# Local attention and gated feed-forward on one core: the first Q/K products on 64x32 tiles from uncast weights, and engine orders given as lists

## The chip, the core and the metric

The kernel runs on one NeuronCore of a Trainium2 chip. The metric is the device time of one execution in microseconds (us); lower is better. A core has TensorE (PE in the profile; PEld is its weight loads), VectorE (DVE), ScalarE (ACT), GpSimd (POOL) and SyncE (SP), each with an instruction stream of its own. They wait for each other through semaphores, and every stream is executed in the order in which it was written. SP and ACT also start DMA transfers here.

## What is computed

The input x has 2048 tokens of 448 values in bfloat16. Four layers follow each other: attention (A), feed-forward (B), and both again with the same weights. Each adds to x what it makes of the layer-normed x. Attention has 16 heads of 28 values; a token looks at itself and at seven tokens before it, two apart. The feed-forward is the product of two projections to 1792 values, projected back, without an activation function.

```python
def _A_ref(x, wqkv, wo):
    B, S, D = x.shape
    H = 16; Dh = D // H
    W, dil = 8, 2
    qkv = (x @ wqkv).reshape(B, S, 3, H, Dh).transpose(2, 0, 3, 1, 4)
    q, k, v = qkv[0], qkv[1], qkv[2]
    ...
    logits = jnp.einsum("bhsd,bhswd->bhsw", q, kg) * Dh ** -0.5
    logits = jnp.where(mask[None, None, :, :], logits, -1e9)
    attn = _softmax(logits, axis=-1)
    o = jnp.einsum("bhsw,bhswd->bhsd", attn, vg)
    return o.transpose(0, 2, 1, 3).reshape(B, S, D) @ wo

def _B_ref(x, w_gate, w_up, w_down):
    return ((x @ w_gate) * (x @ w_up)) @ w_down

x = x + _A_ref(_layernorm(x), wqkv, wo)
x = x + _B_ref(_layernorm(x), w_gate, w_up, w_down)
x = x + _A_ref(_layernorm(x), wqkv, wo)
x = x + _B_ref(_layernorm(x), w_gate, w_up, w_down)
```

## The kernel before

All of x stays in SBUF (`x_sb`), as 16 blocks of 128 tokens, with even tokens in blocks 0 to 7 and odd ones in 8 to 15, so that a token's eight keys are neighbours. Four blocks make a chunk. The names in the code give layer and chunk: `A00` is attention of layer 0, chunk 0; `B10` is the feed-forward of layer 1, chunk 0. `SEQ` lists the jobs: A00 A01 B10 A02 B11 A03 B12 A20 and so on. A chunk of one layer thus overlaps with chunks of others.

**Norm** (`ln_chunk`). For each block VectorE takes statistics (L751, L753), ScalarE the reciprocal root of the variance for two blocks at a time (L754, L756), and VectorE writes the normed block to `xn_sb` (L772). The block then goes, transposed, to `xnTa` (attention) or `xnTb` (feed-forward). For the chunks in `PE_T` (chunks 0, 1 and 2 of layer 0) PE transposes it (L781, four matmuls of 128 columns a block) and ScalarE or VectorE copies it from PSUM (L787). All other blocks are transposed by a DMA that SP issues (L775).

**Q and K** (`qk_chunk`, `twin`, L818). The 448 rows of the contraction are split into seven steps of two 64-row halves; the two halves of a step are two matmuls that PE runs side by side, one for K and one for Q. A unit covers four heads: seven steps, 14 matmuls of 512 columns, into a pair of PSUM banks. Between step 3 and step 4 the halves swap their targets, and a semaphore wait stands there (`crossed`). Four heads of 28 values are spread over 128 columns, 32 a head. The weights therefore aren't used as they lie in HBM. They are staged in `hT`, which the feed-forward needs later only, and cast into `WQK` (L705, 12 copies on ScalarE, VectorE or GpSimd, whichever the scheduler picks). For the two chunks in `FULLQ` (00 and 01) all four units are full; for later chunks the fourth Q group lies in the gaps of the other columns, and a small DMA per 28 rows (`QX`) moves it into place. ScalarE or VectorE copies the pair to `qk` (L872).

**Attention** goes by groups of 240 queries. V is made by the same `twin` (L818) and copied (L925). Scores are 64 small matmuls of 28 rows by 64 columns (L958); ScalarE takes the exponent (L970), VectorE or GpSimd multiplies by a mask (L979). The second product is 64 matmuls on tiles of 64 rows by 32 columns (L997). Its sums come along as a 29th row, are spread by VectorE (L1021 to L1024) and inverted on ScalarE (L1026, L1027); VectorE multiplies (L1047) into `oT`. The output product (`y_blocks`, L834) is added to x by VectorE (L1065).

**Feed-forward** (`b_chunk`). Gate and up are two matmuls side by side, seven steps for 128 of the 1792 values (L1095). ScalarE copies the gate (L1101), VectorE multiplies it with up (L1104) into `hT`, and the down product (L834) is added to x. The last blocks of the last chunk use whole 128-row matmuls (L1116).

**Loads.** At the start SP and ACT issue chunk 0 of x in two loads of 224 KB, WV and the Q/K weights in four pieces each; SP then issues the other three chunks of x, wo, and gate, up and down weights, each load of these last three waiting for the one before it. While nothing else can run, PE executes warm-up products on zeroed data (L692), 18 first of all and 30 at lowest priority.

**What sets the order.** Every operation is added to a list with engines it may run on, an estimate of its duration, what it depends on and a priority. `Sched.schedule` then plays the kernel through with these estimates: an engine that is free takes the ready operation with the best priority, and PE also asks for free PSUM banks. What comes out is a fixed instruction stream for each engine. `TUNE` shifts the priority of most of the 1372 operations, and ties some to an engine:

```python
shift, eng = TUNE.get(op.idx, (0.0, -1))
op.prio += shift
if eng >= 0:
    op.engs = (self.ENGS[eng],)
```

Of the kernel before, what the change touches and what calls it, by code (L numbers as in the profile page):

```python
# [8 lines left out]
D = 448  # L9
H = 16  # L10
DH = 28
# [18 lines left out]
PE_T = ("00","01","02")  # L30
# [9 lines left out]
WQK_ENGS = ("act", "dve", "pool")  # L40
# [6 lines left out]
TUNE = {  # L47
# [229 lines left out]
class Sched:  # L277
    ENGS = ("pe", "act", "dve", "pool", "sp")
    PE_LAT = 200.0
    TO_PE = 22.0  # L280
    LAT = 35.0
    SAME = 30.0
    SELF_LAT = 180.0
    TAIL = {"pe": 0.0, "act": 112.0, "dve": 90.0, "pool": 80.0, "sp": 0.0}
    BEGIN = {"pe": 1120.0, "act": 820.0, "dve": 900.0, "pool": 800.0, "sp": 800.0}
    SWITCH = 175.0
# [289 lines left out]
def build(nc, A_x, A_wqkv, A_wo, B_w_gate, B_w_up, B_w_down, out):  # L576
# [46 lines left out]
    def one(fn, key=None):  # L623
        return [(fn, key)]
# [630 lines left out]
```

## Time and profile before

| what | value |
|---|---|
| median of 3 runs | 395.74 us (395.45 to 395.81) |
| the profiled execution | 395.34 us |
| its span, first to last instruction | 393.5 us |
| PE busy | 383.4 us (97%) |
| VectorE busy | 268.7 us (68%) |
| ScalarE busy | 182.8 us (46%) |
| GpSimd busy | 8.9 us (2%) |
| moved by DMA | 21.74 MB |

Rows of the profile name the line, the engine, the operation and what it writes from what (`ps` is PSUM), then how many. A pair of numbers ahead of a row is its start and its length in us. In brackets or behind an arrow stands what ended the idle time before it. A matmul's shape, such as 64*128, is rows by columns of the tile of the array that it uses. PE's matmuls are pipelined, so a row's length includes the drain of its last matmul, and the mean of one is longer than the distance between two.

### The profile page before, as it was taken

The numbers are of one execution on the slowest core, as the hardware profiler recorded it, in microseconds if no ns is written. First come the engines' busy times: TensorE is split into PE (matmuls) and PEld (weight loads), VectorE is DVE, ScalarE is ACT, GpSimd is POOL, SyncE is SP. The second block draws the span as 40 slices with busy tenths as digits, with TensorE's granted clock in tenths as the row PEclk, the third lists the DMA queues.
The fourth block names the chain that finished last, engine by engine and source line by source line (L and its number), as shares of the span: only waits on it lengthen the run. The fifth ranks groups of instructions, "written<-read, shape, count | busy, mean of one in ns | idle before, by whom it ended". The sixth has DMA issues, their size and how long they took to land.

```text
span 393.5 us, 12725 instructions
## 1 busy us (share of the span) xinstructions
PE 383.4 (97%) x5678; PEld 208.5 (53%) x5678; DVE 268.7 (68%) x577; ACT 182.8 (46%) x297; POOL 8.9 (2%) x29
## 2 busy tenths in 40 slices
PE   8999978999999999999999989999999999999997
PEld 6545544445545454455445545577545555544555
DVE  5996999997996375367874678843689893244323
ACT  4788775554536442464334543333646442134110
POOL 6110000000000000000000000000000000000000
DMA  8645473524230072000330002510003204100002
GB/s 273 189 91 132 109 110 105 85 49 50 48 42 15 13 97 55 2 13 4 66 68 16 16 3 50 72 28 13 27 26 72 27 2 93 45 5 2 23 2 72
DMA packets 50766, 21.74 MB, mean 55 GB/s; under 512 B 41912, under 2 KB 49816, under 8 KB 50712
## 3 DMA queue, kind: packets, MB, share of 16 engines
q1 hardware_dynamic: 49720, 19.95, 25.5%
q8 instruction: 45, 0.74, 0.8%
q10 hardware_dynamic: 992, 0.98, 0.7%
q14 instruction: 9, 0.07, 0.1%
HBM read 8.43 MB, written 1.84 MB: 26 GB/s over the span
## 4 chain that ended last, share of the span: by engine, by line
PE 92%; DVE 3%; DMA 2%; issue 1%; ACT 1%; ACTq 0%
PE ps L1095 43%; PE ps L834 26%; PE ps L818 16%; PE ps L958 2%; PE ps L997 2%; PE ps L1116 1%; DMA hT<-in_A_wqkv_dram 1%; DMA xnTb<-xn_sb 1%; DVE xn_sb L772 1%; DVE hT L1104 1%; ACT g_sb L1101 0%; ACTq L631 0%; DVE E_sb L979 0%; PE ps L781 0%; DVE qk L872 0%
## 5 line engine op out<-in xcount | busy, mean ns | idle before, releaser
L1095 PE MATMUL ps<-xnTb,WGU 64*128 64x512 bf16 x1568 | 178.4, 376 | 1.2 <-DMA xnTb<-xn_sb 0.9
L1095 PEld LDWEIGHTS ps<-xnTb,WGU 64*128 64x128 bf16 x1568 | 85.1, 94 | 84.5 <-issue 6.1
L1101 ACT ACTIVATE g_sb<-ps 128x512 bf16<-128x512 f32 x112 | 66.0, 596 | 110.2 <-PE ps L1095 86.4
L1104 DVE TENSOR_TENSOR hT<-g_sb,ps 128x512 bf16<-128x512 bf16 x112 | 75.8, 683 | 53.6 <-ACT g_sb L1101 50.6
L834 PE MATMUL ps<-WD,hT 64*128 64x448 bf16 x840 | 85.5, 349 | 0.1
L834 PEld LDWEIGHTS ps<-WD,hT 64*128 64x128 bf16 x840 | 43.9, 94 | 35.5 <-DVE hT L1104 0.6
L1065 DVE TENSOR_TENSOR x_sb<-x_sb,ps 128x448 bf16<-128x448 bf16 x62 | 35.8, 614 | 26.2 <-PE ps L834 26.2
L818 PE MATMUL ps<-xnTa,WQK 64*128 64x512 bf16 (+1 forms) x448 | 47.7, 356 | 0.0
L970 ACT ACTIVATE E_sb<-ps 128x1024 bf16<-128x1024 f32 (+1 forms) x36 | 33.6, 977 | 14.3 <-PE ps L958 13.9
L772 DVE TENSOR_SCALAR xn_sb<-x_sb,mv,rstd 128x512 bf16<-128x512 bf16 (+1 forms) x64 | 35.5, 581 | 6.2 <-ACT rstd L756 6.1
L751 DVE BATCH_NORM_STATS2 st<-x_sb 128x6 f32<-128x448 bf16 x64 | 37.4, 611 | 2.3 <-DMA x_sb<-in_A_x_dram 2.3
L818 PEld LDWEIGHTS ps<-xnTa,WQK 64*128 64x128 bf16 x448 | 23.5, 94 | 19.4 <-DVE qk L872 0.5
L834 PE MATMUL ps<-wo_g,oT 64*128 64x448 bf16 x256 | 30.5, 350 | 1.5 <-issue 1.5
L818 PE MATMUL ps<-WV,xnTa 64*128 64x448 bf16 (+1 forms) x252 | 28.5, 340 | 0.7 <-DVE hT L1104 0.4
L872 ACT ACTIVATE qk<-ps 128x1024 bf16<-128x1024 f32 (+1 forms) x23 | 21.5, 948 | 14.0 <-PE ps L818 13.9
L754 ACT ACTIVATE lnv<-mv,eps_sb 128x2 f32<-128x2 f32 x32 | 9.5, 300 | 32.7 <-DVE mv L753 32.7
L979 DVE TENSOR_TENSOR E_sb<-E_sb,MK 128x1024 bf16<-128x1024 bf16 (+2 forms) x39 | 23.2, 610 | 1.3 <-ACT E_sb L970 1.2
L1047 DVE TENSOR_TENSOR oT<-ps,R_sb 128x448 bf16<-128x448 f32 (+2 forms) x38 | 21.0, 597 | 2.8 <-ACT R_sb L1027 2.7
L1026 ACT ACTIVATE R_sb<-R_sb 128x960 f32<-128x960 f32 (+1 forms) x18 | 17.3, 961 | 11.4 <-DVE R_sb L1024 11.4
L872 DVE CAST qk<-ps 128x1024 bf16<-128x1024 f32 (+1 forms) x9 | 9.9, 1102 | 16.1 <-PE ps L818 16.1
L834 PEld LDWEIGHTS ps<-wo_g,oT 64*128 64x128 bf16 x256 | 12.6, 94 | 12.8 <-issue 1.9
L818 PEld LDWEIGHTS ps<-WV,xnTa 64*128 64x128 bf16 x252 | 12.2, 94 | 10.8 <-PE ps L818 1.6
(45 smaller groups left out, 179.2 us busy)
## 6 DMA issues: line engine op xcount, KB each, us to landing
out_dram<-x_sb SPq DMA_DIRECT2D x15, 112.0 KB, 1.7
WGU<-in_B_w_gate_dram SPq DMA_DIRECT2D x7, 224.0 KB, 3.4
WGU<-in_B_w_up_dram SPq DMA_DIRECT2D x7, 224.0 KB, 3.7
WD<-in_B_w_down_dram SPq DMA_DIRECT2D x14, 112.0 KB, 2.1
x_sb<-in_A_x_dram SPq DMA_DIRECT2D x3, 448.0 KB, 7.1
qk<-qk SPq DMA_DIRECT2D x24, 28.0 KB
xnTb<-xn_sb SPq DMA_TRANSPOSE x32, 3.1
hT<-in_A_wqkv_dram SPq DMA_DIRECT2D x2, 224.0 KB, 5.2
```

What stands on the lines that cost most here:

```text
L751: sc.add("dve", one(lambda E, B=B: E.bn_stats(st6[:, B, :], x_sb[:, B, :]), ("bn", li, B)), 525.0, deps=[("x", li - 1, B)] + ([("xn", li - ...
L772: sc.add("dve", one(lambda E, B=B, dst=dst, src=src: E.tensor_scalar(dst, src, mv[:, B, 0:1], rstd[:, B:B + 1], ALU.subtract, ALU.mult), ( ...
L818: parts[0 if s < 3 else 1][1].append((lambda E, w=w, c=c, lo=lo, st=st, sp_=sp_: E.matmul(u["out"](w), u["lhs"](w, c, lo, lo + 64), u["rhs ...
L834: ins.append((lambda E, w=w, c=c, lo=lo, st=st, sp_=sp_: E.matmul(outs(w), lhs(w, c, lo), rhs(w, c, lo), start=st, stop=sp_), keys[w] if s ...
L872: return E.activation(dst, src, ACT.Copy) if hasattr(E, "activation") else E.tensor_copy(dst, src)
L970: return E.activation(E_sb[:, slot, 2 * hp:2 * hp + 2, 0:w], ps[:, b0:b0 + 2, 0:w], ACT.Exp, scale=SCALE)
L979: return E.tensor_tensor(e, e, m, ALU.mult)
L1047: return E.tensor_tensor(dst, src, rec, ALU.mult)
L1065: sc.add("dve", one(lambda E: E.tensor_tensor(x_sb[:, B, :], x_sb[:, B, :], ps[:, bk[w], 0:D], ALU.add), ("x", li, B)), dve_est(D), deps=[ ...
L1095: ins.append((lambda E, u=u, k=k, w=w: E.matmul(u["out"](w), WGU[64 * w:64 * w + 64, k, 128 * u["fc"]:128 * u["fc"] + 128], X[64 * w:64 * ...
L1101: sc.add("act", one(lambda E, gs=gs, bk=bk: E.activation(g_sb[:, gs, 0:n], ps[:, bk[0], 0:n], ACT.Copy), ("G", li, jp, fc)), act_est(n), d ...
L1104: sc.add("dve", one(lambda E, gs=gs, bk=bk, fc=fc: E.tensor_tensor(hT[:, fc, hs, h0:h1], g_sb[:, gs, 0:n], ps[:, bk[1], 0:n], ALU.mult), ( ...
```

## The change

1. For chunks 00 and 01 the Q/K products take their weights from the staging area. Each matmul of a step becomes four on tiles of 64 rows by 32 columns: 28 columns of one head and the first four of the next, whose results no one reads. A unit has 56 matmuls in place of 14, with the same seven steps. These units wait for the staged weights and not for the casts. The end of the staging area gets four zeroed columns.
2. The 12 casts, now for later chunks only, wait for the normed block 3, have a priority of their own, and may run on ScalarE and VectorE but not on GpSimd. `WQK` loses its eighth column group.
3. Chunk 0 of x comes in four loads of 112 KB, one block each, two on SP and two on ACT.
4. Chunk 2 of layer 0 is transposed by DMA (`PE_T` has two chunks).
5. The scheduler's model of PE gets a delay for instructions that aren't fetched yet (`fetch_delay`); some estimates and latencies change.
6. `TUNE` is empty. `ORDER` gives, for each engine, the complete list of operations in the order to execute; the scheduler only works out the banks and checks that each can run.
7. Buffers that are overwritten wait for all of their readers, where they waited for the last unit's.

In the new streams PE has 41 warm-up products ahead of the first transpose (35 before), then 1, 1 and 5 between and behind the transposes of chunk 0. It has 5998 matmuls in all, for 5678: 448 on 64x32 tiles stand for 112, and 16 transposes are gone. VectorE gets five casts directly after the fourth normed block and the copy of one transposed block.

```diff
-PE_T = ("00","01","02")
+PE_T = ("00", "01")
-WQK_ENGS = ("act", "dve", "pool")
+WQK_ENGS = ("act", "dve")
+WQK_P = -18.6
...
-TUNE = {
...
+TUNE = {}
+ORDER = {
+    "pe": [
+        37, 38, 39, 40, 41, 42, 43, 44, 45, 46, 47, 48, 49, 50, 51, 52, 53, 54, 55, 56, 57, 58, 59, 60, 61, 62, 63, 64, 65, 66, 67, 68, 69, 70, 71, 72,
+        73, 74, 75, 76, 77, 142, 145, 78, 151, 79, 148, 80, 81, 82, 83, 84, 229, 221, 223, 222, 219, 224, 217, 220, 218, 175, 169, 172, 166, 230, 232,
...
+    ASK, NEED, FETCH = 164, 440, 2500.0
...
+    def fetch_delay(self, now, est, n):
+        a, self.fetched = self.fetched, self.fetched + n
+        z, late = self.fetched, 0.0
+        k = int((a - self.NEED) // 256) + 1
+        while k >= 0 and 256 * k + self.NEED < z:
+            if k in self.arrive and 256 * k + self.NEED >= a:
+                late = max(late, self.arrive[k] - (now + late + est * (256 * k + self.NEED - a) / n))
+            k += 1
+        k = max(0, int((a - self.ASK) // 256) + 1)
+        while 256 * k + self.ASK < z:
+            if k not in self.arrive:
+                ask = now + late + est * max(0.0, 256 * k + self.ASK - a) / n
+                self.arrive[k] = max(ask + self.FETCH, self.arrive.get(k - 1, 0.0) + 1300.0)
+            k += 1
+        return late
...
+                if ORDER:
+                    op = self.ops[ORDER[e][len(order[e])]] if len(order[e]) < len(ORDER[e]) else None
+                    if op is None or op not in pend[e] or self.ready_at(op, e) > now + 1e-6:
+                        continue
...
-    load_x(0, (0, 1, 2), "sp", 2400.0, -60)
-    load_x(0, (1, 2, 2), "act", 3000.0, -60)
+    load_x(0, (0, 1, 4), "sp", 2400.0, -60)
+    load_x(0, (1, 2, 4), "act", 2400.0, -60)
+    load_x(0, (2, 3, 4), "sp", 2800.0, -59.9)
+    load_x(0, (3, 4, 4), "act", 2800.0, -59.9)
...
+    sc.add("pool", one(lambda E: E.memset(stage[:, 8 * D:8 * D + 4], 0.0), "c_stg"), 100, prio=-45)
...
-            sc.add(WQK_ENGS, one(fn, ("wqk", c, w)), dict(zip(("act", "dve", "pool"), ests)), deps=[("stg", c), "c_wqk0"], prio=-28)
+            sc.add(WQK_ENGS, one(fn, ("wqk", c, w)), dict(zip(("act", "dve", "pool"), ests)), deps=[("stg", c), ("xn", 0, 3)], prio=WQK_P)
...
+                for b in range(u.get("cols", 0)):
+                    ins.append((lambda E, w=w, c=c, lo=lo, st=st, sp_=sp_, b=b: E.matmul(
+                        u["out"](w)[32 * b:32 * b + 32], u["lhs"](w, c, lo, lo + 64)[b], u["rhs"](w, c, lo, lo + 64), start=st, stop=sp_, tile_position=(lo, 32 * b)),
+                        u["keys"][w] if sp_ and b == 3 else None))
...
             def lhs(which, dc, lo, hi):
+                if full:
+                    o = 2 * D * dc + (0 if which else D) + 4 * DH * c
+                    return [stage[lo:hi, o + DH * b:o + DH * b + 32] for b in range(4)]
                 return WQK[lo:hi, dc, c if halved else 4 * which + c, :]
...
-            return dict(bk=bk, out=out, lhs=lhs, rhs=rhs, n=n, deps=WQKR, keys=(("Kps", li, j, c), ("Qps", li, j, c)), c=c)
+            return dict(bk=bk, out=out, lhs=lhs, rhs=rhs, n=n, deps=[("stg", k) for k in range(4)] + ["c_stg"] if full else WQKR, keys=(("Kps", li, j, c), ("Qps", li, j, c)), c=c, **({"cols": 4} if full else {}))
...
-            readersA.setdefault((li, B), []).extend([("Kps", li, j, 3), ("Qps", li, j, 3)])
+            readersA.setdefault((li, B), []).extend([(n, li, j, c) for c in range(4) for n in ("Kps", "Qps")])
```

More of the change, by code (lines that the diff above doesn't have):

```diff
@@ L46 @@
 FILL = 30
-TUNE = {
[172 rows of a table removed]
+TUNE = {}
+ORDER = {
[15 rows of a table added]
+    ],
+    "act": [
[12 rows of a table added]
+    ],
+    "dve": [
[20 rows of a table added]
+    ],
+    "pool": [
+        23, 31, 24, 32, 27, 21, 28, 29, 19, 25, 26, 20, 33, 34, 30, 22, 35, 36,
+    ],
[6 rows of a table added]
+    ],
 }
@@ L394, in schedule @@
                 best = None
+                if ORDER:
+                    op = self.ops[ORDER[e][len(order[e])]] if len(order[e]) < len(ORDER[e]) else None
+                    if op is None or op not in pend[e] or self.ready_at(op, e) > now + 1e-6:
+                        continue
+                    if op.acquire is not None and self.pick_banks(op.acquire, now) is None:
+                        continue
+                    best = op
                 cands = []
-                for op in pend[e]:
+                for op in () if ORDER else pend[e]:
                     r = self.ready_at(op, e)
@@ L460, in schedule @@
                     mode = op.mode
+                    est += self.fetch_delay(now, est, 2 * len(op.ins))
                 op.start, op.end = now, now + est
@@ L597, in build @@
     qk = sb([128, 2, 4, S], bf, "qk")
-    WQK = sb([128, 4, 8, 128], bf, "WQK")
+    WQK = sb([128, 4, 7, 128], bf, "WQK")
     WV = sb([128, 4, D], bf, "WV")
@@ L800, in crossed @@
                 xid[0] += 1
-                tags = [("cross", xid[0], h) for h in (0, 1)]
-                ins = ins[:-2] + [(fn, [t] + ([k] if k is not None else [])) for (fn, k), t in zip(ins[-2:], tags)]
+                tags = [("cross", xid[0], h) for h in range(2 * cols)]
+                ins = ins[:-2 * cols] + [(fn, [t] + ([k] if k is not None else [])) for (fn, k), t in zip(ins[-2 * cols:], tags)]
                 nextk = tags
@@ L1102, in b_chunk @@
                        deps=[("Gps", li, jp, fc), prev], release=[(bk, 0)], prio=prio)
-                war = hslot_users.get((hs, "prev"), WQKR)
+                war = hslot_users.get((hs, "prev"), STGR)
                 sc.add("dve", one(lambda E, gs=gs, bk=bk, fc=fc: E.tensor_tensor(hT[:, fc, hs, h0:h1], g_sb[:, gs, 0:n], ps[:, bk[1], 0:n], ALU.mult), ("H", li, jp, fc)), dve_est(n),
                        deps=[("G", li, jp, fc), ("Ups", li, jp, fc)] + war, release=[(bk, 1)], prio=prio)
-        xslot_users[hs] = (xslot_users[hs] if part == "b" else []) + [("Gps", li, jp, FC - 1), ("Ups", li, jp, FC - 1)]
+        xslot_users[hs] = (xslot_users[hs] if part == "b" else []) + [(n, li, jp, fc) for fc in range(FC) for n in ("Gps", "Ups")]
         users = []
```

53 lines of the change are left out of this document (28 added, 25 removed), and 222 rows, old and new, of tables (ORDER, TUNE).

## The prediction

> **What bounds the kernel now.** I read the page first, then TensorE's busy time by stretches, then its waits, then the start in order of time.
>
> ```profile
> span 393.5 us, 12725 instructions
> PE 383.4 (97%) x5678; PEld 208.5 (53%) x5678; DVE 268.7 (68%) x577; ACT 182.8 (46%) x297; POOL 8.9 (2%) x29
> ```
>
> TensorE (PE) is busy for 97% of the span. A gain must come from work taken off PE, from the time before its first useful product, or from its pauses. The stretches (length, then busy time and count of each engine, granted clock, DMA) size these three:
>
> ```profile
> 11.26:60.77 49.51, 45.81 (x1042) 24.29 (x1043) 44.27 (x113) 39.74 (x61) 1.27 (x1) 1.00 0.55 119
> 60.77:391.10 330.33, 328.01 (x4572) 177.33 (x4572) 217.04 (x446) 137.76 (x226) 0.00 (x0) 1.00 0.21 38
> 11.26:391.10 379.84, 373.82 (x5614) 201.62 (x5614) 261.31 (x558) 177.50 (x286) 1.27 (x1) 1.00 0.25 48
> 391.10:393.50 2.40, 0.01 (x1) 0.00 (x0) 0.39 (x1) 0.00 (x0) 0.00 (x0) 1.00 0.23 72
> ```
>
> So the span is 11.26 us of start, 373.8 us of PE work, 3.7 us of pauses up to the first gate product (60.77), 2.3 us of pauses after it, and a tail of 2.4. The profiled execution took 395.34 us, 1.84 more than its span, and 0.4 less than the median of 395.74. The pauses by cause:
>
> ```profile
> PE ps L834 <- issue: 1.5, 1, 1.5
> PE ps L958 <- DVE E_sb L979: 1.4, 1, 1.4
> PE ps L1095 <- DMA xnTb<-xn_sb: 0.9, 1, 0.9
> PE ps L997 <- DVE v_sb L925: 0.8, 1, 0.8
> ```
>
> Three of the four belong to one place, 53 to 61 us, where VectorE is late with masks, V and the norm of layer 1. VectorE is busy 44.27 of 49.51 us in that stretch: it is PE's close second there, and everything I claim about the start must pass it.
>
> **The start, part by part.** Before, it goes so:
>
> ```profile
> 1.12 6.86 PE L692 MATMUL ps<-warm 128*128 128x256 bf16 x35 [1.12 <-DVE warm L663]
> 1.32 0.93 SPq L631 DMA_DIRECT2D WV<-in_A_wqkv_dram  x2
> 4.34 1.15 DVE L751 BATCH_NORM_STATS2 st<-x_sb 128x6 f32<-128x448 bf16 x2 [2.33 <-DMA x_sb<-in_A_x_dram]
> 6.59 0.30 DVE L753 BATCH_NORM_AGGREGATE mv<-st 128x2 f32<-128x6 f32 x2
> 6.81 0.70 DVE L772 TENSOR_SCALAR xn_sb<-x_sb,mv,rstd 128x512 bf16<-128x512 bf16 x2
> 7.43 0.27 DVE L705 COPY WQK<-hT 128x448 bf16<-128x448 bf16 x1
> 7.61 0.71 ACT L705 ACTIVATE WQK<-hT 128x112 bf16<-128x112 bf16 x1 [0.87 <-DMA hT<-in_A_wqkv_dram]
> 7.63 3.43 POOL L705 COPY WQK<-hT 128x448 bf16<-128x448 bf16 x6 [2.53 <-DMA hT<-in_A_wqkv_dram]
> 8.60 1.54 DVE L772 TENSOR_SCALAR xn_sb<-x_sb,mv,rstd 128x512 bf16<-128x512 bf16 x2 [0.90 <-ACT rstd L756]
> 10.07 0.73 DVE L787 COPY xnTa<-ps 128x512 bf16<-128x512 bf16 x2
> 10.20 0.40 PE L781 MATMUL ps<-ident,xn_sb 128*128 128x128 bf16 x4
> 13.73 4.91 PE L818 MATMUL ps<-xnTa,WQK 64*128 64x512 bf16 x44
> 18.57 1.07 PE L781 MATMUL ps<-ident,xn_sb 128*128 128x128 bf16 x16
> ```
>
> *x in four loads.* The 112 KB loads of WD landed a median 2.1 us after issue, the first 224 KB of x after 3.5:
>
> ```profile
> WD<-in_B_w_down_dram SPq DMA_DIRECT2D x14, 112.0 KB, 2.1
> x_sb<-in_A_x_dram SPq DMA_DIRECT2D x1, 224.0 KB, 3.5
> hT<-in_A_wqkv_dram ACTq DMA_DIRECT2D x2, 224.0 KB, 5.5
> ```
>
> Block 0 thus lands 0 to 1.4 us earlier; I take 0.7, the middle, as two loads still share the engines. Each queue issues one load more, so WV, the staged weights and x chunks 1 to 3 issue about 0.47 us later (0.93 for two issues). The staged weights then land by about 3.3 + 5.5 = 8.8 us; that must beat PE's need, below.
>
> *Casts out of the way.* The pair of norms at 8.60 waited for a reciprocal root behind ScalarE's first cast, and ran at 0.77 us each while GpSimd copied (the earlier pair: 0.35 each). Without casts the four norms follow each other: statistics from 3.6, 2.5 us for four blocks as before, then four norms of 0.35. They end near 7.6, not 10.15.
>
> *But PE does not come then.* Its order is fixed: 41 warm-up products now stand ahead of the first transpose, not 35.
>
> ```profile
> L692 PE MATMUL ps<-warm 128*128 128x256 bf16 x27 | 5.9, 420 | 1.1 <-DVE warm L663 1.1
> ```
>
> That row covers the first 6.8 us: 27 products at 0.21 us spacing, their slow phase, though the code plans 18. The other eight of the 35 fit the rest at about 0.11. So 41 end at 1.12 + 27 x 0.212 + 14 x 0.107 = 8.3 us. Sixteen transposes at 1.07/16 and two warm-ups between them take 1.3 us, to 9.7. The last transposed block is copied by VectorE (0.4 us) to about 10.3; five warm-ups and six V products fill the time. The useful stream begins at about 10.25 instead of 11.26: **-1.0 us**. The weights (8.8) are there. Most of the 2.5 us that the norms win is lost to warm-ups.
>
> *First products on 64x32 tiles.* A unit was 14 matmuls, two row halves by seven steps; now each is four matmuls of 32 columns, 56 in all. Before, 44 matmuls took 4.91 us, 22 steps of 0.22. The nearest rows for 64x32 tiles are the attention's second product:
>
> ```profile
> L997 PE MATMUL ps<-E_sb,v_sb 64*32 64x64 bf16 x1024 | 10.9, 195 | 0.8 <-DVE v_sb L925 0.8
> ```
>
> and from the chain that ended last (start, length, how many):
>
> ```profile
> 22.24 2.26 PE ps L818 x20
> ...
> 27.41 0.27 PE ps L997 x32
> ...
> 31.03 0.61 PE ps L997 x64
> ...
> 40.65 0.76 PE ps L834 x8
> ...
> 44.89 0.64 PE ps L958 x64
> ```
>
> Twenty full products took 2.26 us, two at a time, so one alone streams 512 columns in 0.226. Thirty-two matmuls of 72 columns, one after another, would need 32 x 72/512 x 0.226 = 1.02 us; they took 0.27: nearly four run at once, at least. Eight pairs of load and matmul issue in 8 x 0.61/64 = 0.076 us, well inside a step of 0.22. So the step stays at 0.22 us if all eight tiles stream together, and doubles if only four do: 0 to +12.3 us for the 56 steps of two chunks. I take +0.3, nearest to the row, whose 0.27 us is set by issue as much as by streaming; no row shows a limit at four.
>
> [...]
>
> *Chunk 2 transposed by DMA.* Sixteen PE transposes go: **-1.0 us** (18.57 row), and with them four PSUM copies. SP issues four transposes instead, as it does for chunk 3 (the second row is the landing of those four):
>
> ```profile
> 24.78 3.95 SPq L775 DMA_TRANSPOSE xnTa<-xn_sb  x3
> DMA to landing us min/median/max: 2.4/3.6/5.2
> ```
>
> They take 1.3 us each to issue, queued among the gate and up loads. The changed order asks for chunk 2 after about 16.4 us of PE work, at 27 us. VectorE's last norm of that chunk comes near 23.5, and such transposes landed 2.4 to 5.2 us after issue: 26 to 28.7, a pause of 0 to 1.7. I put 0.5 of it into the pauses below.
>
> *The casts, moved.* Twelve casts now follow the fourth norm on ScalarE and VectorE alone. VectorE gets five at once, about 1.3 us (its one before took 0.27), after the copy that ends at 10.3. Its statistics of chunk 1 begin at 11.5, not 10.72: VectorE loses 0.8 us where PE wins 1.0. GpSimd's one mask goes to VectorE too, and is in the count below.
>
> *The orders.* From there the lists decide.
>
> ```profile
> 10.72:55.17 44.45, 42.51 (x952) 22.57 (x950) 39.21 (x102) 36.37 (x58) 1.61 (x2) 1.00 0.51 120
> 56.46 4.07 DMA xnTb<-xn_sb
> ```
>
> Before, VectorE worked 39.2 us from the statistics of chunk 1 (10.72) to the fourth layer-1 norm (55.17), and idled 5.2; that norm's DMA transpose took 4.1, and the first gate product came at 60.77. The changed order has nearly the same work on VectorE in between, 91 instructions for 92: gone are four half masks and a half Q/K copy (about 1.9 us), new are a mask, a cast and two output products split off (1.8). So the norm ends at 11.5 + 39.1 = 50.6 without idling, 55.8 with the old idle time. I take a quarter of it, 51.9, since the masks, V and sums come to VectorE earlier while it still has norms to do; that choice weighs most in the sum. The gate product can then start at 51.9 + 4.1 + 0.2 = 56.2.
>
> PE's work ahead of it in the new order, by the chain's rows: 56 steps of 64x32 (12.3), 16 transposes (1.1), 84 + 28 products with cast weights, full and half (11.1), 84 + 14 V products (8.6), 48 output products (4.6), scores and second products (6.2), together 43.9 us. With 0.8 us of pauses on the way, PE is there at 10.25 + 43.9 + 0.8 = 55.0 and waits 1.2. The pauses up to there are 2.0 us (3.7 before), **-1.7**.
>
> Behind it PE is full, as before.
>
> ```profile
> 231.10 0.71 PE L958 MATMUL ps<-qk 28*64 28x64 bf16 x64
> 231.73 0.68 PE L997 MATMUL ps<-E_sb,v_sb 64*32 64x64 bf16 x64
> ...
> 234.59 0.55 PE L834 MATMUL ps<-wo_g,oT 64*128 64x448 bf16 x3 [1.46 <-issue]
> ```
>
> The 1.5 us "issue" pause stands in the middle of a stage, behind 128 short products: its next instructions weren't there. The fetch model moves such bursts apart; the gain is 0 to 1.5, and the change adds 320 matmuls to fetch. I take 1.2 left of 2.3, **-1.1**. The order ends on the same 42 products: the tail costs the same. The other edits (semaphores, latencies, wider waits for buffers long read) cost nothing while PE's work covers them; the lists already contain their effect.
>
> **Sum:** 395.34 - 1.0 - 1.0 - 1.7 - 1.1 + 0.3 = 390.8 for a profiled execution like this one; the 0.4 up to the median stays inside the range.
>
> **Rivals.**
>
> *Half the tiles wait (slower).* If moving data or PSUM writes let only four of eight tiles stream, each of 56 steps costs 0.22 more: 390.8 + 12.0 = 402.8. It decides from 4.8/56 = 0.09 us a step on. For it: no row has 512 columns on such tiles. Against: the 72-column row already reaches four, limited by issue. 10%.
>
> *Weight loads show.* If a tile's load waits for the matmul in that tile, a step grows by up to eight pairs' issue, 0.076 us: +4.3 in place of 0.3, 394.8. Steps with two halves hide their loads entirely (PE's busy time is full of products, PEld's 53% lies beside it), which speaks against. [...] 10%.
>
> *VectorE is the bound.* With its old 5.2 us of idling the fourth norm ends at 55.8, the gate product starts at 60.0, and PE's remaining 328.9 us (373.8 - 1.0 - 43.9), 1.2 of pauses, tail and 1.84 give 394.3: most of the gain is given back at layer 1. For it: 44.27 of 49.51 busy, and a later start of chunk 1. Against: what it waits for comes earlier. 14%.
>
> *The orders miss.* The lists have no slack; one more pause such as the present 1.5 in each of three layers would give 395.3. 8%.
>
> **Chances.** Forecast 58% (388.6 to 393). Its low end: no idling on VectorE (-1.2) and the warm-ups' slow phase shorter by a third (27 to 18 products, -1.0). The high end, 395.3, takes in VectorE, the exposed loads and the missed orders, and leaves out the doubled step. 0.2% (0.8 us) is about what a measurement of this kernel can tell from no change. Faster by more (below 394.95): forecast, 11 of VectorE's 14 and 7 of the 18 in the two cases near 395, 76%; within it: 3 and 6, 9%; slower: 5 and the 10, 15%.
>
> **What would show it.** PE's first V product near 10.2 and its first 64x32 product near 10.5, behind a 41-long row of warm-ups; 224 products of chunk 0 in about 6.2 us (12 would mean four tiles, 8.3 exposed loads); 16 transposes fewer; the first gate product at 55 to 57; no long "issue" pause. I am wrong if 64x32 steps exceed 0.3 us, or if the first gate product comes after 59.

## The result, and the profile after

The kernel after takes a median of 398.75 us (395.66 to 401.89, 20 runs), the kernel before beside it 395.75 us (394.38 to 397.47, 20 runs): a ratio of 1.0064, 95% interval 1.0042 to 1.0087, slower. The ratios compare fast runs alone (one of after's 20 was slow), so they are not the quotient of the medians. In a later comparison (a_again, below) the same kernel came to 1.001 (0.9982 to 1.0038), which can't be told from no change. The forecast was 390.8. The profiled execution took 396.55 us, at the lower end of the spread; what it shows explains about 6 of the 8 us missed, and the spread is a part of the answer.

The page of after, first:

```profile
span 394.8 us, 13338 instructions
PE 384.1 (97%) x5998; PEld 206.0 (52%) x5998; DVE 268.6 (68%) x581; ACT 179.7 (46%) x296; POOL 4.1 (1%) x22
```

PE's busy time is 384.1 us for 383.4, although 16 transposes are gone. The stretches of after (length, then busy time and count of each engine, granted clock, DMA), cut at the same events as those of before; the last row is VectorE's way from the statistics of chunk 1 to the fourth layer-1 norm:

```profile
9.19:61.22 52.03, 47.16 (x1363) 25.23 (x1364) 46.10 (x120) 40.52 (x64) 0.00 (x0) 1.00 0.65 135
61.22:392.40 331.18, 328.92 (x4572) 174.32 (x4572) 216.87 (x446) 135.52 (x225) 0.00 (x0) 1.00 0.20 39
392.40:394.80 2.40, 0.00 (x0) 0.00 (x0) 0.31 (x1) 0.00 (x0) 0.00 (x0) 1.00 0.23 72
10.54:54.62 44.08, 41.26 (x1170) 21.83 (x1156) 38.91 (x100) 35.59 (x58) 0.00 (x0) 1.00 0.62 131
```

The span is 9.19 us of start, 47.16 of PE work and 4.87 of pauses (52.03 - 47.16) up to the first gate product, 328.92 and 2.26 behind it, and 2.40 of tail. The start won 2.07 us on before (11.26), and at the first gate product they were gone: 61.22 for 60.77. The waits of PE in after (what waited, for what; us in total, times, longest):

```profile
PE ps L1025 <- DMA xnTb<-xn_sb: 1.9, 1, 1.9
PE ps L761 <- issue: 1.3, 2, 1.0
...
PE ps L927 <- issue: 0.9, 2, 0.6
PE ps L744 <- issue: 0.6, 2, 0.4
PE ps L888 <- issue: 0.5, 1, 0.5
```

"issue" is a pause with nothing in the profile that it waits for. Before had one, of 1.46 us; after has seven, 3.2 us in sum, five of them (2.0) ahead of the gate product. Four of the lines of the start, and how the stretch ends (start, length, engine):

```profile
1.12 6.41 PE L612 MATMUL ps<-warm 128*128 128x256 bf16 x41 [1.12 <-DVE warm L583]
3.38 1.15 DVE L672 BATCH_NORM_STATS2 st<-x_sb 128x6 f32<-128x448 bf16 x2 [1.37 <-DMA x_sb<-in_A_x_dram]
9.62 4.29 PE L744 MATMUL ps<-xnTa,hT 64*32 64x512 bf16 x150
14.07 2.33 PE L744 MATMUL ps<-xnTa,hT 64*32 64x512 bf16 x74 [0.16 <-issue]
...
52.67 4.95 SPq L696 DMA_TRANSPOSE xnTb<-xn_sb  x3
53.24 1.39 DVE L693 TENSOR_SCALAR xn_sb<-x_sb,mv,rstd 128x896 bf16<-128x896 bf16 x2 [0.59 <-ACT rstd L677]
...
61.22 1.04 PE L1025 MATMUL ps<-xnTb,WGU 64*128 64x512 bf16 x8 [1.86 <-DMA xnTb<-xn_sb]
```

The fourth layer-1 norm ends at 54.63 (53.24 + 1.39). SP needs 4.95 us for the last three transposes, so the fourth starts 1.7 us after its norm (56.3); the gate product comes 6.6 us after it. One of these issues took 2.27 us, where the least was 1.23 (nanoseconds from shortest to longest, then the first and the last start):

```profile
L696 SPq DMA_TRANSPOSE xnTb<-xn_sb x4: 1227/1264/2271, 49.4 to 56.3; - x4
```

### The profile page after: what moved, and what is told of

Read it like the earlier page. It is cut to its first block, busy times and chain, and to the rows that moved or that the text cites. A ratio compares the mean times of both kernels' runs of the same rounds, so it can differ in the third digit from the quotient of the medians.

```text
span 394.8 us, 13338 instructions
## 1 busy us (share of the span) xinstructions
PE 384.1 (97%) x5998; PEld 206.0 (52%) x5998; DVE 268.6 (68%) x581; ACT 179.7 (46%) x296; POOL 4.1 (1%) x22
## 3 DMA queue, kind: packets, MB, share of 16 engines
HBM read 8.43 MB, written 1.84 MB: 26 GB/s over the span
## 4 chain that ended last, share of the span: by engine, by line
PE 93%; DVE 2%; ACT 2%; issue 1%; DMA 1%
PE ps L1025 43%; PE ps L761 26%; PE ps L741 12%; PE ps L744 3%; PE ps L927 2%; PE ps L888 2%; PE ps L612 2%; PE ps L1046 1%; DMA xnTb<-xn_sb 1%; DVE hT L1034 1%; PE ps L702 0%; ACT g_sb L1031 0%; ACT v_sb L855 0%; DVE x_sb L995 0%; DVE E_sb L909 0%
## 5 line engine op out<-in xcount | busy, mean ns | idle before, releaser
L1025 PEld LDWEIGHTS ps<-xnTb,WGU 64*128 64x128 bf16 x1568 | 83.6, 94 | 87.1 <-issue 6.4
L1034 DVE TENSOR_TENSOR hT<-g_sb,ps 128x512 bf16<-128x512 bf16 x112 | 75.0, 682 | 61.7 <-ACT g_sb L1031 60.0
L761 PE MATMUL ps<-WD,hT 64*128 64x448 bf16 x840 | 86.9, 349 | 1.5 <-issue 1.3
L741 PE MATMUL ps<-xnTa,WQK 64*128 64x512 bf16 (+1 forms) x336 | 35.9, 350 | 0.3
L741 PEld LDWEIGHTS ps<-xnTa,WQK 64*128 64x128 bf16 x336 | 16.7, 94 | 15.5 <-PE ps L741 1.8
L956 ACT ACTIVATE R_sb<-R_sb 128x960 f32<-128x960 f32 (+1 forms) x18 | 17.3, 960 | 7.0 <-DVE R_sb L954 6.9
L957 ACT ACTIVATE R_sb<-R_sb 128x960 f32<-128x960 f32 (+1 forms) x18 | 17.2, 958 | 0.3
```

The lines of the kernel that those rows point to most:

```text
L741: ins.append((lambda E, w=w, c=c, lo=lo, st=st, sp_=sp_: E.matmul(u["out"](w), u["lhs"](w, c, lo, lo + 64), u["rhs"](w, c, lo, lo + 64), s ...
L761: ins.append((lambda E, w=w, c=c, lo=lo, st=st, sp_=sp_: E.matmul(outs(w), lhs(w, c, lo), rhs(w, c, lo), start=st, stop=sp_), keys[w] if s ...
L1025: ins.append((lambda E, u=u, k=k, w=w: E.matmul(u["out"](w), WGU[64 * w:64 * w + 64, k, 128 * u["fc"]:128 * u["fc"] + 128], X[64 * w:64 * ...
L1034: sc.add("dve", one(lambda E, gs=gs, bk=bk, fc=fc: E.tensor_tensor(hT[:, fc, hs, h0:h1], g_sb[:, gs, 0:n], ps[:, bk[1], 0:n], ALU.mult), ( ...
```

## What an issue pause is: theory and rivals

I counted PE's matmuls ahead of each issue pause (the count of PE in the stretch from 0 to the pause). Of after, then of f2_shift_after (below):

```profile
0.00:14.05 14.05, 12.75 (x220) 8.96 (x221) 9.76 (x31) 5.84 (x15) 4.14 (x22) 1.00 0.74 237
0.00:31.23 31.23, 28.38 (x729) 17.57 (x729) 24.32 (x72) 20.60 (x42) 4.14 (x22) 1.00 0.68 172
0.00:34.98 34.98, 31.42 (x856) 19.06 (x856) 27.40 (x77) 23.82 (x46) 4.14 (x22) 1.00 0.66 167
```

```profile
0.00:25.14 25.14, 22.80 (x602) 15.94 (x603) 18.94 (x63) 15.37 (x32) 4.14 (x22) 1.00 0.67 190
0.00:37.27 37.27, 32.17 (x984) 20.70 (x984) 27.29 (x77) 25.26 (x47) 4.14 (x22) 1.00 0.59 161
```

A matmul is two instructions, load and product (x5998 of PE and x5998 of PEld in after's page). 220 matmuls are 440 instructions; 602, 729, 856 and 984 are 1204, 1458, 1712 and 1968, that is 440 + 3, 4, 5 and 6 times 256, less 4 to 8 (probably the instructions of PE that are no matmuls). The other issue pauses of 0.2 us or more that I counted in the first 45 us stand within 10 instructions of such a number too: 474 matmuls (948) in after, 601 (1202) in f1_shift_before, 730 (1460) in f2_shift_after and e1_wide, 600 (1200) in i1_wide162 and i2_wide78. Later ones fall further short, by about one in 100 to 120: after's at 3391 and 3897 matmuls by 58 and 70 instructions, before's at 3767 by 74. The page of after shows 47 packets on the queue "q8 instruction", 0.77 MB, 16 KB each, and PE has 11996 such instructions, 46.9 times 256; before has 45 packets for 44.4 times 256, m1_fetch 61 for 60.3. So PE's code comes in blocks of 256 instructions here, and a pause is PE at the end of a block, waiting for the next.

**Theory:** a block takes a time of its own; code that uses up 256 instructions faster makes PE wait, and that delays everything behind it, VectorE too. **Rivals:** 64x32 products cost more by themselves; the weights' loads slow the blocks down; VectorE's chain ends as late whatever PE does; adjacent halves of one unit expose their wait.

## The experiments

Lines such as 396.83 (394.68 to 401.06, 12) give median, range and number of runs; the ratio is to before on the same chip, with its 95% interval.

**a_again**: after, unchanged.

> The changed kernel once more, for a second profile and more times. Fetch theory: PE's instructions come in blocks of 256; the changed kernel's first profile shows pauses put down to issue at 13.9, 22.9, 26.7, 30.7 and 34.4 us, one block apart each, so the second profile shows pauses at the same instructions, of other lengths (2 us together in the first), and a slower execution has longer ones. Order theory: the lists have no slack, so a slower execution shows longer waits for VectorE, ScalarE and DMA and the same issue pauses. Either way the median is 398 to 399.

396.83 (394.68 to 401.06, 12), 1.001 (0.9982 to 1.0038), below the 398 to 399 that both theories gave. Its profiled execution (399.66) paused at five of the first one's seven products, for other times, and behind the pause at the gate product the granted clock (the column ahead of the last two) fell:

```profile
14.99 2.33 PE L744 MATMUL ps<-xnTa,hT 64*32 64x512 bf16 x74 [1.06 <-issue]
...
32.57 0.42 PE L888 MATMUL ps<-qk 28*64 28x64 bf16 x33 [1.11 <-issue]
```

```profile
62.00:64.00 2.00, 1.47 (x10) 0.71 (x12) 0.99 (x2) 0.00 (x0) 0.00 (x0) 0.71 0.29 72
64.00:66.00 2.00, 2.00 (x12) 0.86 (x10) 0.00 (x0) 0.56 (x2) 0.00 (x0) 0.50 0.52 135
```

The pause behind product 220 took 0.16 and 1.06 us in two executions of one program, so what a block end costs varies. This span is 3.1 us longer than the first one: 1.3 of it is there at the gate product (62.53 for 61.22), and 1.7 are lost at half clock.

**e1_wide**: after without 64x32 tiles.

```diff
-return [stage[lo:hi, o + DH * b:o + DH * b + 32] for b in range(4)]
+return stage[lo:hi, o:o + 128]
```

> The changed kernel with one product of 64x128 in place of four of 64x32 in the first two chunks, on 128 neighbouring uncast columns; heads don't lie at multiples of 32 then, so the output is not the reference's. Lists, loads and everything else as changed. Fetch theory: issue pauses in the first 60 us all but vanish (2.0 us), steps take 0.22 us again in place of 0.24 (1.4 us), the spread shrinks to that of the kernel before, and the median falls to 393.5 to 395. Order theory: only the 1.4 us of the steps go, the spread stays: 397 to 397.5.

397.03 (395.22 to 401.01, 12), 1.0035 (1.0001 to 1.0069): no gain, where the fetch theory gave 393.5 to 395 and the order theory 397 to 397.5. The groups of Q/K products ahead of the gate product, after and e1_wide (count | busy us, mean ns):

```profile
L744 PE MATMUL ps<-xnTa,hT 64*32 64x512 bf16 x448 | 13.9, 377 | 0.8 <-issue 0.6 <-PE ps L744 0.2
L741 PE MATMUL ps<-xnTa,WQK 64*128 64x512 bf16 x84 | 10.9, 378 | 0.3
```

```profile
L741 PE MATMUL ps<-xnTa,hT 64*128 64x512 bf16 x112 | 13.0, 377 | 0.4 <-DMA hT<-in_A_wqkv_dram 0.3
L741 PE MATMUL ps<-xnTa,WQK 64*128 64x512 bf16 x84 | 10.9, 377 | 0.3
```

So 64x32 tiles cost 0.9 us in all 56 steps. The time is the order theory's, but it doesn't settle the two, because with 672 instructions fewer the block ends fell elsewhere, with pauses of 1.80 (40.97), 0.22 and 1.68 us (290.45).

**e2_narrow** and **e3_late**: before, with 64x32 tiles from cast weights in layer 0 (e2) or layer 2 (e3); the cut, put into `twin`:

```diff
+for q in range(u.get("cols", 0)):
+    ins.append((lambda E, ...: E.matmul(u["out"](w)[32 * q:32 * q + 32], u["lhs"](w, c, lo, lo + 64)[:, 32 * q:32 * q + 32], ...
```

> The kernel before with only the split: the first two chunks' Q/K products as four of 64x32, from the cast weights, every engine's order unchanged. Fetch theory: issue pauses appear between 12 and 35 us (1 to 2 us), steps cost 1.1 to 1.4 us, the spread grows: 398 to 399.5. Order theory: the order of before has slack, at most the steps show: 396 to 397, spread as before.

> The kernel before with the same split in the first two chunks of layer 2 (448 products of 64x32 in place of 112), when few loads run. Fetch theory with loads as the cause of slow fetches: steps cost about 1 us, issue pauses under 0.5 us: 396.5 to 397. If fetches are as slow without loads: pauses of 1 to 2 us in layer 2 as well, 398 to 399. Order theory: 396.5 to 397.

e2_narrow: 401.12 (398.5 to 403.37, 6), 1.0114 (1.007 to 1.0158), 1.6 us over the fetch theory's range, with issue pauses of 0.87, 2.07 and 0.38 us. Its profiled execution (403.37) also lost 5.1 us in three stretches at half clock (granted 0.50), so not all of the loss is pauses. e3_late: 394.93 (394.56 to 397.68, 12), 0.9968 (0.9943 to 0.9992): faster than before, which no theory gave, with the same extra products and no issue pause of 0.15 us or more in its profile. So the tiles alone don't decide. Its 672 instructions moved the end that made before pause at 234.59; whether that gave the gain is what the next two runs ask.

**f1_shift_before** and **g4_shift258**: before, with nothing but more instructions ahead, 162 (27 warm-ups cut) and 258 (43). f2_shift_after, g2_shift78 and g3_shift120 do the same to after, i1 and i2 to e1_wide.

```diff
+[(lambda E, q=q: E.matmul(ps[:, wb[0], 64 * q:64 * q + 64], warm[:, 0:128], warm[:, 64 * q:64 * q + 64], ...)) for q in range(4)] if n < 27 else ...
```

> The kernel before, with 27 of its warm-up products cut into four of 64 columns each: 81 products, 162 instructions more on PE ahead of everything, the same columns streamed, every order unchanged. Block theory: all 'issue' pauses seen so far stand at a multiple of 256 PE instructions, so every block boundary moves 81 products ahead; the 1.46 us pause at 234.6 goes, as it did in e3_late (whose 672 added instructions move the later boundaries by 160 modulo 256), at most a short one (under 0.7 us) appears behind the short products near 33, 97 or 224, and the time is 394.3 to 395.3 with before at 395.9. Rival: the 64x32 tiles of e3_late were worth its gain themselves, or chance was: the pause stays behind the same short products and the time is 395.7 to 396.3.

> The kernel before with 43 warm-up products cut in four: 258 PE instructions more, one whole block. Block theory: all boundaries return to where they were but for two instructions, so the gain of f1_shift_before (162 instructions, 395.1) is lost again: the pause behind the short products of layer 2 (1.46 us at 234.6 in before) is back within 0.5 us of its length and the time is 395.5 to 396.3, but for up to 0.5 us that the slower row of cut warm-ups may cost at the start. Rival, that the cut warm-ups themselves gave f1 its gain (start, clock): the time is 395.1 or less.

f1: 395.11 (394.01 to 395.92, 12), 0.9975 (0.9955 to 0.9995). The pause at 234.6 is gone; one of 0.48 us stands at 34.52, behind 601 matmuls, a block end. g4: 397.94 (395.39 to 447.88, 12), 1.0025 (1.0001 to 1.005). One whole block further on, the pause is back:

```profile
235.54 0.55 PE L834 MATMUL ps<-wo_g,oT 64*128 64x448 bf16 x4 [1.65 <-issue]
```

The block theory's place is shown with that. g4's median is 1.6 us over the range expected; its executions often had a lower granted clock (0.991 or less in seven of twelve), which the cut warm-ups may bring and which I did not follow up.

**f2_shift_after**, **g2_shift78**, **g3_shift120**.

> The kernel after, with the same 81 products added in the warm-up. Block theory: the pauses at 14.1, 31.3, 35.0, 187.4 and 228.1 (at the same products in both profiles of after) are gone from these products and stand 81 products earlier, wherever those lie in a dense stretch; the bursts of 64x32 products hold over three blocks, so some pause stays whatever the shift: 1.5 to 3 us of them in sum, time within 1 us of after's (395.8 to 397.8). Rival, that a pause belongs to the products it stands at (a bank, a weight load, a mode change): the same products pause as before.

> The kernel after with 13 warm-up products cut in four: 78 PE instructions more, boundaries 39 products earlier. Together with a_again (0), f2_shift_after (162) and g3_shift120 this asks whether the loss belongs to the alignment or to the change. If to the alignment: one of the four lies at 393 to 395, below before. If the bursts of 64x32, score and second products are too dense at any alignment: issue pauses of 1.5 us or more in sum ahead of the first gate product in each, and all four lie between 396 and 400.

> The kernel after with 20 warm-up products cut in four: 120 PE instructions more, boundaries 60 products earlier. Expected as for g2_shift78: 393 to 395 if the loss belongs to the alignment and this one is a lucky one, 396 to 400 with issue pauses of 1.5 us or more ahead of the first gate product if the code is too dense at any alignment.

f2: 399.16 (395.93 to 401.56, 11), 1.0075 (1.0044 to 1.0106); g2: 401.01 (398.22 to 401.64, 6), 1.0102 (1.0068 to 1.0136); g3: 400.32 (398.5 to 402.37, 6), 1.0105 (1.0072 to 1.0138). All three medians lie above the ranges expected (up to 397.8 for f2, 400 for g2 and g3). The pauses left the products where after had them and stood at the block ends (f2's rows above), with 3.1, 2.2 and 3.1 us ahead of the layer-1 norms. At none of the four alignments tried does the code get by.

**m1_fetch**: the block's time by itself.

> The fetch measured by itself: the kernel before, with two of its warm-up products (the 20th and 21st) replaced by runs of 1024 products on 64x32 tiles, four tiles in turn, the first run 256 columns wide, the second 64 columns wide. Each run is 2048 PE instructions, eight blocks of 256. By their columns the runs need 1024/4 x 0.113 = 28.9 us and, at the 0.61 us per 64 that such short products took in the trace of before, 9.8 us. Theory that a block takes 3.2 us or more however dense the code is (no two transfers on the instruction queue stood closer than 3.2 us in the traces of before, after, f2_shift_after, e2_narrow and f4_thin): the second run takes 26 to 32 us, with a pause every 128 products; the first 29 to 33 us. Rival, the fetch model's own figures (2.5 us a block, 1.3 us apart): the second run takes 10 to 20 us, the first 28.9. The kernel is longer by what the two runs take; only their profile counts.

One execution, 453.56 us. The two runs of products:

```profile
12.66 7.17 PE L692 MATMUL ps<-warm 64*32 64x256 bf16 x256 [1.61 <-issue]
20.12 16.59 PE L692 MATMUL ps<-warm 64*32 64x256 bf16 x640 [0.29 <-issue]
38.21 1.21 PE L692 MATMUL ps<-warm 64*32 64x64 bf16 x128 [1.50 <-issue]
42.21 1.44 PE L692 MATMUL ps<-warm 64*32 64x64 bf16 x128 [2.79 <-issue]
45.94 1.89 PE L692 MATMUL ps<-warm 64*32 64x64 bf16 x128 [2.29 <-issue]
49.39 1.89 PE L692 MATMUL ps<-warm 64*32 64x64 bf16 x128 [1.56 <-issue]
52.85 1.89 PE L692 MATMUL ps<-warm 64*32 64x64 bf16 x128 [1.56 <-issue]
56.30 1.89 PE L692 MATMUL ps<-warm 64*32 64x64 bf16 x128 [1.56 <-issue]
59.76 1.89 PE L692 MATMUL ps<-warm 64*32 64x64 bf16 x128 [1.56 <-issue]
63.21 3.86 PE L692 MATMUL ps<-warm 64*32 64x64 bf16 x66 [1.56 <-issue]
```

The stretch from 49.39 to 63.21, with the granted clock ahead of the last two columns:

```profile
49.39:63.21 13.82, 7.57 (x512) 7.00 (x512) 0.00 (x0) 0.00 (x0) 0.00 (x0) 0.50 0.02 5
```

Every 128 short products (256 instructions) PE stops. The starts of the last five rows stand 3.455 us apart on average (63.21 - 49.39, by four), 13.5 ns an instruction; PE ran at half clock there and stopped for 1.56 us each time. At first it ran faster, stopped for up to 2.79, and the starts were 4.00 and 3.73 us apart. So a block came every 3.46 to 4.00 us here, whether PE was quick or slow. The DMA engines were all but idle (0.02): a block took that long with no other load beside it. The fetch model's 2.5 and 1.3 us fall. A 64x32 step is 16 instructions, 0.216 to 0.25 us by these distances, against 0.226 us of columns: such steps leave no lead, and the next 128 scores or second products (256 instructions in 1.2 us, at 0.61 us per 64) find nothing in store. A 64x128 step has 4 instructions: a block lasts 14 us (64 steps of 0.22), over three times what the next took to come.

**f4_thin**: do the weights' loads make the blocks late?

```diff
-plain_dma("sp", WGU[lo:lo + 64, k, :], src[64 * k:64 * k + 64, :], ...
+hk = lo + 64 if k == 0 else lo + 1
+plain_dma("sp", WGU[lo:hk, k, :], src[64 * k:64 * k + hk - lo, :], ...
```

> The kernel after, whose gate, up and down weights are loaded in part only: one row in place of 64 or 128 from the third gate/up load and the third down load on (same number of DMAs, about 4 MB less to move in the first 60 us); the products read the loaded slices again in their place, so the output is not the reference's; instructions and orders are unchanged. Theory that instruction blocks arrive late because their transfer shares the DMA engines with the weights: the issue pauses ahead of the first gate product (2.0 us in the first profile, 2.8 in the second) fall below 0.5 us, the runs lie within 2.5 us of each other in place of 6, and the time is 392.5 to 394.5. Rival, that a block takes its 4 us whatever else is moved: the same pauses within 0.4 us each; only the layer-1 transposes can gain, 0 to 1 us: 395.8 to 396.8.

396.12 (394.81 to 399.4, 12), 1.0017 (0.9995 to 1.0038). The start of PE's products:

```profile
10.34 4.29 PE L746 MATMUL ps<-xnTa,hT 64*32 64x512 bf16 x150 [1.10 <-DMA hT<-in_A_wqkv_dram]
16.08 1.27 PE L746 MATMUL ps<-xnTa,hT 64*32 64x512 bf16 x40 [1.45 <-issue]
```

The pause of 1.45 us is no test, since the first load that was cut starts at 17.17, behind it. Of the two later pauses ahead of the norms that both profiles of after have, the one near 36 is as long as there (0.64 for 0.62), and the one near 31 (0.51 and 1.11) is gone. So f4 doesn't settle whether the loads add to a pause; m1_fetch shows blocks that took 3.46 to 4.00 us without them. The first row shows another loss of the early start: PE now reaches the staged weights as they land, and waits 0 to 1.22 us for them, by execution.

**f3_inter**: another unit's half between adjacent halves (seven pairs).

```diff
-270, 266, 267, 268, 248, 391, 392, 300, 395, 396, 283, 253,
+270, 266, 267, 248, 268, 391, 300, 392, 395, 283, 396, 253,
```

> The kernel after, with the PE order changed in layer 0 alone: seven units whose two halves directly follow one another get another unit's half between them (one of 64x32, three of cast Q/K products, one of V, one output, one V late). Theory of adjacent halves: each costs 0.2 to 0.3 us of exposed waiting between halves, so PE's busy time to the first gate product falls by 1.4 to 2.0 us and the time by 1 to 1.7: 395.1 to 395.8 where after is 396.8. Rival, VectorE sets the first gate product (its fourth layer-1 norm ended at 54.6): PE comes earlier and waits longer, 396.3 to 397.0.

399.08 (396.37 to 402.48, 10), 1.0075 (1.0048 to 1.0103): slower, outside both expectations. PE then waits for others, first of all here:

```profile
PE ps L741 <- DVE x_sb L995: 1.3, 1, 1.3
PE ps L888 <- ACT R_sb L957: 0.8, 1, 0.8
```

Swapping seven pairs of neighbours in PE's order made other engines late; the price of adjacent halves isn't measured by this.

**h1_four** and **h2_four_shift**: before with its orders fixed and x chunk 0 in four loads (h2: with f1's cut too).

> The kernel before, with its own orders written out and chunk 0 of x loaded in four parts as in after; casts, 64x128 products and PE transposes stay as in before. It asks whether an earlier start survives to the end where PE's code isn't dense. In after the statistics began at 3.38 in place of 4.34. Theory A (the gain was eaten by instruction blocks and clock): what the start gains here, 0 to 1.0 us (the second pair of norms waited for ScalarE's rstd behind casts, which may take all of it), is still there at the first gate product (60.77 before) and in the time: 394.7 to 395.5, as much as the first V product comes earlier. Rival B (VectorE's chain up to the layer-1 norms takes the gain whatever PE does): the first V product is earlier by 0.3 us or more and the first gate product isn't: 395.6 to 396.1.

> h1_four with 27 warm-up products cut in four as in f1_shift_before: a candidate faster than both kernels. The block boundaries leave the short products of layer 2, worth 0.6 us in f1_shift_before's median. If both gains add: 394.0 to 394.8; if the start's gain is lost on the way: 395.0 to 395.4, as f1_shift_before.

h1: 397.2 (395.5 to 398.39, 12), 1.0018 (0.9996 to 1.004). h2: 396.47 (395.02 to 398.07, 12), 0.9994 (0.9972 to 1.0017). Both medians lie above every range expected. Statistics began at 3.29, but the second pair of norms still stood behind ScalarE's casts, and PE paused longer for it:

```profile
9.06 1.55 DVE L786 TENSOR_SCALAR xn_sb<-x_sb,mv,rstd 128x512 bf16<-128x512 bf16 x2 [0.88 <-ACT rstd L770]
...
9.98 0.40 PE L795 MATMUL ps<-ident,xn_sb 128*128 128x128 bf16 x4 [2.52 <-DVE xn_sb L786]
```

Behind that wait the granted clock was 0.5 from about 10.8 to 14.2, which cost 1.7 us more. Four loads alone showed no gain; the question of the two theories wasn't reached.

**i1_wide162** and **i2_wide78** reach it.

> e1_wide (after with one 64x128 product on 128 contiguous uncast columns in place of four 64x32 ones, so that its output isn't the reference's) with 27 warm-up products cut in four, 162 PE instructions more. It keeps after's early start and orders without the dense 64x32 code, at another place of the block boundaries. Theory A (late blocks and the half clock behind them are what takes the gain): e1_wide without its 3.7 us of issue pauses would take 392.3; with fewer of them here the time follows their sum: 392 to 394 if no issue pause over 0.5 us is left, and no first gate product after 59.5. Rival B (VectorE's chain sets the first gate product): it stays at 60 to 61.5 and the time is 394 to 396 even without issue pauses.

> As i1_wide162 (same part left out), with 13 warm-up products cut, 78 instructions more. Theory A: time = 392.3 plus the issue pauses seen, first gate product before 59.5 where none of 0.5 us or more stands ahead of it. Rival B: first gate product at 60 to 61.5 whatever the pauses; 394 to 396 or more.

i1: 394.7 (392.02 to 395.91, 11), 0.9963 (0.9943 to 0.9983). i2: 396.56 (395.46 to 398.78, 12), 1.0021 (1.0003 to 1.0039). The last norms of layer 1 in i1, then in i2:

```profile
51.69 1.39 DVE L693 TENSOR_SCALAR xn_sb<-x_sb,mv,rstd 128x896 bf16<-128x896 bf16 x2 [0.60 <-ACT rstd L677]
```

```profile
54.82 1.39 DVE L693 TENSOR_SCALAR xn_sb<-x_sb,mv,rstd 128x896 bf16<-128x896 bf16 x2 [0.60 <-ACT rstd L677]
```

With all profiles of after's orders the norm can be set against PE's pauses (the last two columns are the norm's end and what is left of it without the first two):

| run | first Q/K product | issue pauses up to the norm | fourth norm ends | way less pauses |
|---|---|---|---|---|
| after | 9.62 | 1.97 | 54.63 | 43.0 |
| a_again | 9.64 | 2.79 | 55.91 | 43.5 |
| f4_thin | 10.34 | 2.09 | 55.40 | 43.0 |
| f2_shift_after | 10.14 | 3.14 | 56.57 | 43.3 |
| g3_shift120 | 9.92 | 3.07 | 56.27 | 43.3 |
| g2_shift78 | 10.72 | 2.21 | 56.04 | 43.1 |
| e1_wide | 10.23 | 1.80 | 54.19 | 42.2 |
| i1_wide162 | 10.55 | 0.23 | 53.08 | 42.3 |
| i2_wide78 | 10.30 | 2.38 | 56.21 | 43.5 |

The way is the same within 0.5 us for each kind of tile, once the pauses are taken off (i2's 43.5 holds a stretch at a granted clock of 0.5 between 36 and 41, 1.7 us). A late block moves VectorE's norm one for one, and rival B falls: VectorE has no floor of its own at 54 or 60; it idles because PE is late. But i1's time is 0.7 over theory A's range and inside B's, and its first gate product came at 59.57, past A's bound (59.5) and short of B's (60): its profile has 1.22 us of waiting for staged weights at the start, 0.89 of issue pause at 226.62 and 0.70 behind a second product. So theory A holds for the norm, and its figure for the whole was too low. With 64x128 tiles and 1.1 us of issue pauses in its profile, i1 is still 3.9 us above the forecast of 390.8: late blocks, with the tiles and the half clock, are about half of the miss, and the rest lies in the terms below.

Of kernels that compute the whole reference, e3_late and f1_shift_before beat both, by 0.32% and 0.25%; their orders are before's.

## Why the prediction was wrong, point by point

It forecast 390.8 as the likeliest and gave 15% to slower. Its own sign of being wrong came: a first gate product after 59 (61.22).

- **Start, -1.0.** Right in kind, too small: -2.07. The 41 warm-ups took 6.41 us; their slow phase was about 18 products (1.12 + 18 x 0.212 + 23 x 0.107 = 7.4, where the transposes begin), not the 27 that I carried over from before. The low end of the forecast had this in it. The length of that phase differs from execution to execution (the first V product came at 8.78 in f4_thin and at 9.50 in e1_wide), so a part of the 2.07 is luck.
- **Transposes, -1.0, and the tail.** Right as far as the traces show: 16 matmuls of 128 columns are gone, the tail is 2.4. Chunk 2's DMA cost no more than 0.3 us (a_again).
- **64x32 steps, +0.3.** Right in kind, 0.6 too small. Eight tiles stream together: 28 steps of chunk 0 took 6.6 us without its pause, 0.236 a step, and e1_wide prices all 56 at 0.9. Neither half the tiles waited nor did the loads show; those two rivals fall.
- **PE's work ahead of the gate product, 43.9.** 47.16 in after, 3.3 too small. The rows of the chain were a poor ruler: by them before would have had 44.9 (43.9 + 1.0; the 0.3 for the tiles isn't in the 43.9), and had 45.81. Of the other 2.4, 0.9 is the tiles' (e1_wide). The rest is the order's: e1_wide, with no such tiles, still has 46.49 us of work there. What in the order costs it stays open, as f3_inter did not price it.
- **The failed step: "I take a quarter of it, 51.9".** I expected VectorE to lose most of its old 5.2 us of idling, and wrote that this choice weighs most. It idled 5.17 us (44.08 - 38.91). The norm ended at 54.63, and the table says why: 2.0 us of late blocks and a way of 43.0 in place of 41.4 from the first Q/K product (10.5 to 51.9), of which the wide kernels (42.2) give about half to the tiles. The way on to the gate product, 4.1 + 0.2, was also short: 6.6 us, 1.7 of it because SP issues the three transposes one after another; before's own rows had 5.6 (55.17 to 60.77). Together 5.0 us at the gate product.
- **"The fetch model moves such bursts apart", 1.2 us of pauses left behind it.** It failed too: 2.26, and 2.0 of issue pauses ahead of the gate product, where I had seen the "320 matmuls to fetch" and counted nothing for them. The row that I had (one pause of 1.46 us behind 128 short products) already said what a block costs.
- **The rivals.** "VectorE is the bound" (394.3 for the 396.55 of the profiled execution) named the right place, for the wrong reason: VectorE was late because PE's code was. "The orders miss" (395.3) came nearest and named pauses like the 1.5, but laid them to lists without slack. The right rival was missing: one in which the denser code runs into the fetch.

Start -1.06, work +3.26, pauses ahead +2.87 (4.87 for 2.0), pauses behind +1.06: 6.1 us over the 388.7 of span that the forecast's parts add up to. (With the 1.84 they make 390.5; the sum's 390.8 has the tiles' 0.3 besides.) The 2.2 us from there to the median of 20 runs are not in one profile. They fit the varying pauses (0.16 to 1.45 us at one block end) and half-clock stretches of about 3.4 us, 1.7 us each: ten of the other profiles (m1_fetch aside) had a mean granted clock of 0.987 to 0.996, and nine such stretches in seven of them (a_again, e2_narrow, f4_thin, g3_shift120, h1_four, h2_four_shift, i2_wide78) began inside or within 3 us behind a wait of 1.45 to 2.52 us. The clock isn't all of it: eight of after's 20 executions had a granted clock of 1.0 throughout and still took 395.66 to 400.29 us. That the pauses make up the rest wasn't tested.

## What to carry to other kernels

Count PE's instructions, not only its columns: here 256 of them took at least 3.46 us to arrive (m1_fetch), so an operation cut into four is free only where slower code beside it leaves the fetch a lead: the 64x32 products came with 2.0 us of issue pauses ahead of the gate product in after, and with none of 0.15 us or more in e3_late. Before crediting a shorter path, check that no pause of another engine on it is itself an echo of PE's, and take the way from the last link to the consumer from the trace, with the queue that it passes. When a kernel with more instructions changes its time, shift the block ends by some cheap instructions (162 here) and measure again before blaming the operation.

## What the runs showed of the hardware

- PE's code arrived in 16 KB blocks of 256 instructions (47 packets in after, 0.77 MB), one per 3.46 to 4.00 us where PE waited for each (m1_fetch), and PE's first wait came after 440 instructions in after. At the block ends in m1_fetch's run of small matmuls PE stopped for 1.50 to 2.79 us each.
- Behind some pauses the granted clock was 0.5 for about 3.4 us (62.8 to 66.2 in a_again, after 1.90 us of waiting), behind others about as long it stayed 1.0 (after, 1.86 us at 61.22).
